# A recurrent attention kernel with a MoE layer behind it: the old state added on TensorE, the range check gathered at the end, two more slabs inverted by halves, a new tile order, and an issue order read from a table

## The chip, the cores and the metric

One core of one Trainium2 chip. The metric is the device time of one launch in microseconds (us). The kernel before takes 695.13 us, the median of three runs (693.57 to 698.21).

## The reference

For each of 4 x 8 batch heads a state of 40 x 40 is carried over 768 steps, then a normalised two-layer block with a residual follows on the 320 joined channels of each position:

```python
for t in range(S):
    y[:, :, t] = einsum('bhd,bhde->bhe', rt, state)
    Sa = einsum('bhde,bhe->bhd', state, at)
    state = state * wt[:, :, None, :] - einsum('bhd,bhe->bhde', Sa, bt) + einsum('bhd,bhe->bhde', vt, kt)
xn = (x - mu) / sqrt(var + 1e-6) * g_ln          # x: y of all heads, [4, 768, 320]
out = x + maximum(xn @ w_ch1, 0) @ w_ch2         # 320 -> 1280 -> 320
```

## The kernel before

The 768 positions are 24 chunks of 32; all 32 batch heads of a chunk are worked on together. Seven **slabs** group the chunks: 0-1, 2-3, 4-7, 8-11, 12-15, 16-19, 20-23.

**prep(c)** loads the chunk's decays and inputs (`load_e`, L332, two transfers of some 450 KB into `wa` and `bk`), forms the running products of the decays with two scans on DVE (`gE` L356, `qE` L365), multiplies `aT` (L373) and `bk` (L387) by them, checks the range of the decays (`wild`, L345), transposes `qE` (pq, L398) and multiplies all pairs of positions (`tri`, L412); the product, masked on DVE (`gk`, L419), goes to DRAM (`d_g`). **invert(slab)** reads a slab's triangles back, one per partition, solves them by substitution in 30 steps (or, for slabs in `HALVES`, two halves side by side in 14), each step a multiply and an add (L465, L471, L475), and stores the result (`d_tt`). Slabs 0 to 2 are inverted on DVE, 3 to 6 on POOL.

**chain(c)** is the recurrence: prh (L549, needs the state), a copy `hv` on ACT, solve (L564, with the slab's inverse `tt`; in chunks of `HALVES` three solves with a copy between, the middle one with `nn`), four copies `u` into `x` (L579) and one into `ub`, then st (L596): the update of the state in two PSUM banks. Four DVE additions (L606) add the old state while they move it to the other state buffer, and for 12 of the 23 next chunks, those where the frame of the products starts anew, four more DVE instructions scale it (L614). ss (L628) transposes the state. **post(c)** makes the outputs: ut (L653), z (L672) and its mask on DVE (L681), y (L693), `xt` (L701). After each odd chunk, **norm(g)** (statistics on DVE and ACT, transposes nt, L874) and **moe(g)** follow for 256 positions: ten first-layer blocks of 8 matmuls (L925), each followed by a relu on ACT (`hh`, L930) and a remainder on DVE (`hl`, L934), and twenty second-layer blocks of 3 matmuls (L902). A pair of chunks and its MoE block are called a pair below; there are 12.

tri and z take their matmuls in groups of four: the operands stand in two halves of the rows (`HROW`), the results go to two halves of the columns.

**The order.** Every step is entered as a task with an assumed duration and with what it reads and writes. `Plan.run` lays all tasks on the five engines in one pass of list scheduling: whichever ready task has the earliest due time goes next, MoE blocks get due times 37 us apart (`PERIOD`), and where PE has nothing ready between 6 and 70 us of the plan, it gets a filler matmul (`unit`, L1036). The instructions are then emitted in that order, engine by engine; each engine runs its own in order. All transfers are issued by SP's queue, in order.

```python
        by_time = sorted(order)
    with tc.manual_schedule():
        for at, _, t, b in by_time:
            if t is unit:
                unit(b)
            else:
                t["emit"](t["on"], b)
```

After the last task the collected range check is folded (L1052, L1054, L1058, L1060) and read by all engines; only if a decay was out of range a slow loop runs, which it does not here.

Of the kernel before, what the change touches and what calls it, by code (L numbers as in the profile page):

```python
# [11 lines left out]
F32 = mybir.dt.float32  # L12
# [20 lines left out]
HALVES = (0, 1)  # L33
BY_POOL = (3, 4, 5, 6)
NBK = 7
NPI = 10
NXT = 5

PERIOD, END = 18.5, 500.0
STRETCH = 1.5  # L40
UNITS = (6.0, 70.0)
BACKLOG = 2.0
RATE = 270.0


class Plan:

    ENGINES = ("PE", "DVE", "ACT", "POOL", "SP")  # L50
    READ = {"PE": 0.28, "DVE": 0.09, "ACT": 0.11, "POOL": 0.12}
# [26 lines left out]
    def run(self, n_banks=8, unit=None):  # L78
        T = self.tasks
        n = len(T)  # L80
        follow = [[] for _ in T]
        left = [0] * n
        uses = {}
        opens = {k: t for t in T for k in t["bank"]}
        for t in T:
            for k in t["ps"]:
                o = opens[k]
                if o is not t:
                    o["deps"].update(d for d in t["deps"] if d < o["n"])
        for t in T:  # L90
            for d in t["deps"]:
                follow[d].append(t["n"])
            left[t["n"]] = len(t["deps"])
            t["uses"] = set()
        for t in T:
            for k in t["bank"]:
                uses[k] = 0
        for t in T:
            for k in t["ps"]:
                uses[k] += 1  # L100
        free = {e: 0.0 for e in self.ENGINES}
        ready = {e: [] for e in self.ENGINES}
        ends = [None] * n
        avail = [0.0] * n
        done = [False] * n
        banks = list(range(n_banks))
        held = {}
        count = {"moe": 0, "po": 0, "small": 0}
        cap = {"moe": 2, "po": 2, "small": 5}
        wire = [0.0]  # L110
        events = []
        order = []
        now = 0.0

        def release(t):
            for e, us in t["where"]:
                heapq.heappush(ready[e], (t["key"], t["n"]))

        for t in reversed(T):
            us = min(u for _, u in t["where"])  # L120
            if t["where"][0][0] == "SP":
                us = 0.45 + t["kb"] / RATE + t["land"] + 1.0
            else:
                us = us * STRETCH + 0.3
            late = t["due"] if t["due"] is not None else min((T[f]["late"] for f in follow[t["n"]]), default=END)
            t["late"] = late - us
            t["key"] = t["late"] + t["shift"]
        for t in T:
            if left[t["n"]] == 0:
                release(t)  # L130
        events.append(0.0)
        n_done = 0
        back = []
        while n_done < n:
            while back and back[0][0] <= now + 1e-9:
                heapq.heappush(banks, heapq.heappop(back)[1])
            moved = True
            while moved:
                moved = False
                for e in self.ENGINES:  # L140
                    if free[e] > now + 1e-9 or e == "SP" and wire[0] > now + BACKLOG:
                        continue
                    put = []
                    got = None
                    q = ready[e]
                    while q:
                        k, i = heapq.heappop(q)
                        t = T[i]
                        if done[i]:
                            continue  # L150
                        if avail[i] > now + 1e-9:
                            put.append((k, i))
                            continue
                        if t["bank"]:
                            s = t["sort"] or "small"
                            if len(banks) < len(t["bank"]) or count[s] + len(t["bank"]) > cap[s]:
                                put.append((k, i))
                                continue
                        got = t
                        break  # L160
                    for x in put:
                        heapq.heappush(q, x)
                    if got is None:
                        if e == "PE" and unit and UNITS[0] <= now < UNITS[1] and banks:
                            order.append((now, len(order), unit, heapq.nsmallest(1, banks)[0]))
                            free[e] = now + 0.3
                            heapq.heappush(events, free[e])
                        continue
                    t, i = got, got["n"]
                    us = dict(t["where"])[e]  # L170
                    done[i] = True
                    n_done += 1
                    for k in t["bank"]:
                        s = t["sort"] or "small"
                        count[s] += 1
                        held[k] = (heapq.heappop(banks), s)
                    t["on"] = e
                    t["at"] = now
                    order.append((now, len(order), t, {k: held[k][0] for k in t["ps"]}))
                    free[e] = now + us  # L180
                    if e == "SP":
                        start = max(wire[0], now + us)
                        wire[0] = start + t["kb"] / RATE
                        heapq.heappush(events, wire[0] - BACKLOG + 1e-3)
                        end = wire[0] + t["land"]
                    else:
                        end = now + us
                    t["end"] = end
                    heapq.heappush(events, free[e])
                    heapq.heappush(events, end)  # L190
                    for k in t["ps"]:
                        uses[k] -= 1
                        if not uses[k]:
                            b, s = held[k]
                            count[s] -= 1
                            heapq.heappush(back, (end + 0.1, b))
                            heapq.heappush(events, end + 0.1)
                    for f in follow[i]:
                        left[f] -= 1
                        lag = 0.0 if e == "SP" else self.READ[e]  # L200
                        fe = T[f]["where"]
                        if len(fe) == 1 and fe[0][0] == e:
                            lag = 0.0 if e != "PE" else 0.0
                        if e == "SP":
                            lag = 0.1
                        avail[f] = max(avail[f], end + lag)
                        if not left[f]:
                            heapq.heappush(events, avail[f])
                            release(T[f])
# [981 lines left out]
```

## Time and profile before

| | |
|---|---|
| median of three runs | 695.13 us |
| the profiled execution, its own time | 701.11 us |
| its span (first to last instruction) | 699.4 us |
| mean granted TensorE clock, as a share of 2.4 GHz | 0.82 |
| busy: PE, DVE, ACT, POOL | 588.6, 433.7, 280.1, 254.6 us |
| moved by DMA | 92.13 MB |

Matmuls are pipelined, so PE's busy time includes latencies that overlap; the distance from the start of one group to the start of the next says what a group costs. The granted clock of a stretch is 1.00 at 2.4 GHz and 0.50 at 1.2 GHz. A matmul of full fp32 stands as two records in the trace and as one instruction in the program.

### The profile page before, as it was taken

How to read it: one execution, taken by the hardware profiler on the slowest of the kernel's cores; microseconds unless marked ns; L12 is line 12 of the kernel's file. 1: busy time of each engine (PE TensorE's matmuls, PEld its weight loads, DVE VectorE, ACT ScalarE, POOL GpSimd, SP SyncE). 2: the span in 40 equal slices, each digit the busy share in tenths (PEclk: the TensorE clock that was granted, in tenths of full speed). 3: DMA queues.
4: the chain of work that ended last, by engine and by line, in shares of the span. 5: the costliest groups of instructions: out<-in, count | busy, mean ns of one | idle time of the engine just before them, and what ended most of it. 6: DMA issues, size and time to landing. Idle time of an engine off the chain costs nothing.

```text
span 699.4 us, 29631 instructions
## 1 busy us (share of the span) xinstructions
PE 588.6 (84%) x13160; PEld 535.1 (77%) x13160; DVE 433.7 (62%) x923; ACT 280.1 (40%) x672; POOL 254.6 (36%) x357
## 2 busy tenths in 40 slices
PE   7998777479979779699798888897896998989976
PEld 6897676368868679599688787796795987969865
DVE  7798967699977657654585656654436355263422
ACT  7432336623334533443524424423425335253321
POOL 8427522452149923088411157711088000000000
PEclk9999865559989769869699699697697795977969
DMA  8898679644393765563566556256424242050100
GB/s 250 211 240 184 183 184 223 188 131 123 109 190 92 198 145 176 157 154 84 155 145 176 131 119 192 69 125 168 85 60 134 54 146 63 18 149 1 34 1 23
DMA packets 90549, 92.13 MB, mean 132 GB/s; under 512 B 55728, under 2 KB 70064, under 8 KB 90416
## 3 DMA queue, kind: packets, MB, share of 16 engines
q1 hardware_dynamic: 90416, 90.18, 50.0%
q8 instruction: 105, 1.72, 1.1%
q14 instruction: 28, 0.23, 0.1%
HBM read 71.11 MB, written 19.05 MB: 129 GB/s over the span
## 4 chain that ended last, share of the span: by engine, by line
PE 66%; DVE 21%; issue 7%; ACT 2%; DMA 2%; SPq 0%; DVEq 0%; ACTq 0%
PE ps L925 17%; PE ps L902 14%; PE ps L564 4%; PE ps L412 4%; PE ps L672 4%; PE ps L549 3%; PE ps L1036 3%; PE ps L628 3%; PE ps L693 3%; DVE x L614 2%; PE ps L596 2%; PE ps L398 2%; PE ps L521 2%; PE ps L874 2%; PE ps L653 2%
## 5 line engine op out<-in xcount | busy, mean ns | idle before, releaser
L925 PE MATMUL ps<-xh,w 128*128 128x256 f32 x480 | 123.1, 317 | 4.7 <-DVE xl L882 1.8
L930 ACT ACTIVATE hh<-ps 128x256 fp32r<-128x256 f32 x120 | 46.1, 385 | 173.1 <-PE ps L925 172.2
L934 DVE SCALAR_TENSOR_TENSOR hl<-ps,hh 128x256 fp32r<-128x256 f32 x120 | 50.1, 421 | 100.9 <-ACT hh L930 100.5
L902 PE MATMUL ps<-w,hh 128*128 128x320 f32 x480 | 111.6, 318 | 0.0
L925 PEld LDWEIGHTS ps<-xh,w 128*128 128x128 f32 x480 | 95.4, 219 | 7.3 <-ACT xh L878 2.2
L387 POOL TENSOR_TENSOR bk<-bk,gE 112x1024 f32<-112x1024 f32 x24 | 56.8, 2369 | 75.9 <-DMA d_g<-gk 22.7
L902 PEld LDWEIGHTS ps<-w,hh 128*128 128x128 f32 x480 | 77.3, 188 | 1.7
L925 PE MATMUL ps<-xl,w 128*128 128x256 f32 x240 | 74.8, 311 | 0.0
L902 PE MATMUL ps<-w,hl 128*128 128x320 f32 x240 | 74.0, 308 | 0.0
L475 POOL TENSOR_TENSOR yi<-yi,ytmp 128x30 f32<-128x30 f32 (+14 forms) x120 | 65.7, 547 | 9.4
L471 POOL TENSOR_TENSOR ytmp<-yi 128x30 f32<-128x30 f32 (+14 forms) x120 | 65.3, 544 | 8.6
L681 DVE TENSOR_TENSOR x5s<-ps,mask 64x256 f32<-64x256 f32 x96 | 40.5, 422 | 37.7 <-PE ps L672 35.9
L1036 PE MATMUL ps<-start,ident 128*128 128x160 f32 x318 | 54.7, 330 | 8.6 <-DVE gk L419 5.4
L373 POOL TENSOR_TENSOR aT<-wa,qE 112x512 f32<-112x512 f32 x21 | 27.3, 1302 | 94.0 <-DVE qE L365 43.1
L527 ACT COPY xk<-ps 64x320 f32<-64x320 f32 x96 | 40.4, 420 | 45.3 <-PE ps L521 44.0
L1036 PEld LDWEIGHTS ps<-start,ident 128*128 128x128 f32 x318 | 49.6, 211 | 10.4 <-DVE gk L419 5.9
L925 PEld LDWEIGHTS ps<-xl,w 128*128 128x128 f32 x240 | 52.7, 219 | 0.6 <-DVE xl L882 0.5
L606 DVE TENSOR_TENSOR x<-ps,x 40x320 f32<-40x320 f32 x92 | 45.0, 489 | 7.5 <-PE ps L596 5.5
L635 ACT COPY xk<-ps 40x320 f32<-40x320 f32 x92 | 38.6, 420 | 17.4 <-PE ps L628 11.3
L902 PEld LDWEIGHTS ps<-w,hl 128*128 128x128 f32 x240 | 45.1, 188 | 0.0
L628 PE MATMUL ps<-ident,x 40*104 40x40 f32 x368 | 30.8, 249 | 15.9 <-DVE x L614 14.4
L628 PEld LDWEIGHTS ps<-ident,x 40*104 40x104 f32 x368 | 25.5, 154 | 24.1 <-DVE x L614 10.5
(115 smaller groups left out, 1138.4 us busy)
## 6 DMA issues: line engine op xcount, KB each, us to landing
rvu<-in_rv_dram SPq DMA_DIRECT2D x24, 672.0 KB
wa<-in_et_dram SPq DMA_DIRECT2D x24, 455.4 KB
bk<-in_et_dram SPq DMA_DIRECT2D x24, 448.0 KB
d_g<-gk SPq DMA_DIRECT2D x48, 128.0 KB
x<-in_vt_dram SPq DMA_DIRECT2D x48, 128.0 KB
d_a<-aT SPq DMA_DIRECT2D x24, 231.0 KB
x2s<-d_a SPq DMA_DIRECT2D x48, 99.0 KB
x5s<-in_r_dram SPq DMA_DIRECT2D x48, 96.0 KB
```

Source lines behind the costliest of these rows:

```text
L387: (nc.gpsimd if e == "POOL" else nc.vector).tensor_tensor(out=kb, in0=kb, in1=ge[R, :, 0:C].unsqueeze(2).broadcast_to([112, 16, 2, C]), op ...
L471: g.tensor_tensor(out=tv, in0=y[:, j + 1:, j:j + 1].broadcast_to([n, m, j]), in1=y[:, j:j + 1, 0:j].broadcast_to([n, m, j]), op=ALU.mult)
L475: g.tensor_tensor(out=yv, in0=yv, in1=tv, op=ALU.add)
L527: nc.scalar.copy(out=xk[c % 2][64 * pp:64 * pp + 64, pp, 4 * z:4 * z + 4], in_=banks[b[name]][64 * pp:64 * pp + 64].rearrange("p (i f x) - ...
L606: nc.vector.tensor_tensor(out=x2[n][bs, pp, hf, :, 0:D], in0=banks[b[names[pp]]][64 * hf:64 * hf + D, 0:CH].rearrange("p (h e) -> p h e", ...
L628: nc.tensor.transpose(out=banks[b[name]][0:104, D * k:D * k + D], in_=X2[bs, pp, hf, 2 * h:2 * h + 2].rearrange("p h e -> p (h e)")[:, 0:104],
L681: nc.vector.tensor_tensor(out=x5s[zs, pp].rearrange("p f h t -> p (f h) t")[:, par::2], in0=banks[b[f"pz{c}_{par}"]][zs, 0:256].rearrange( ...
L902: nc.tensor.matmul(banks[b[name]][:, 0:CH], lhsT=l[:, us], rhs=ws[f"w2_{f}"][:, y], start=f == 0 and x == 0, stop=f == 9 and x == 2)
L925: nc.tensor.matmul(ph, lhsT=l, rhs=r, start=x == 0, stop=x == 7)
L930: nc.scalar.activation(out=hhs[n], in_=banks[b[name]][:, 0:256], func=AF.Relu)
L934: nc.vector.scalar_tensor_tensor(out=hls[n], in0=banks[b[name]][:, 0:256], scalar=0.0, in1=hhs[n].bitcast(F32), op0=ALU.max, op1=ALU.subtract)
L1036: nc.tensor.matmul(banks[b][:, 0:160], lhsT=ident, rhs=flat(start0)[:, 0:160], start=True, stop=True)
```

## The change

- The state's old value is added in PSUM by TensorE: `se` multiplies it by the identity into the two banks of st before st accumulates there. What DVE did in L606 becomes a copy on ACT or DVE, or, in frame chunks, one DVE multiplication from PSUM that replaces L606 and L614.
- The range check leaves prep: at the end eight transfers of 480 KB (`ww`, all decays once more) and eight DVE instructions do it for all chunks, folded and flagged inside the ordered part.
- Slabs 2 and 3 (chunks 4 to 11) are inverted by halves.
- `aT`, `bk`, the inversion steps and some weight conversions may be put on DVE or POOL each; the conversions get buffers of their own.
- tri and z take their four tiles in the order of `TILES`.
- `Plan.run` is gone; the order, the engine of each task and its PSUM banks are read from a table of 2,689 words. It has no filler matmuls.

```diff
-HALVES = (0, 1)
-BY_POOL = (3, 4, 5, 6)
+HALVES = (0, 1, 2, 3)
-NPI = 10
+NPI = 8
+TILES = ((0, 0), (1, 1), (1, 0), (0, 1))
 class Plan:
-    def run(self, n_banks=8, unit=None):
...
+    def listed(self, table):
         held = {}
...
+        for word in table.split():
+            n = word.rstrip("0123456789")
+            if n == "u":
+                yield None, "PE", int(word[1:])
+                continue
+            cut = next(i for i, x in enumerate(word) if x.isalpha())
+            t = self.tasks[int(word[:cut])]
+            held.update(zip(t["bank"], map(int, word[cut + 1:])))
+            yield t, self.ENGINES[word[cut]], {k: held[k] for k in t["ps"]}
...
-        task(both, a_, r=[kw, kq], w=[("aT", c % 2)], of="aT")
+        task([("DVE", 0.68), ("POOL", 1.18)], a_, r=[kw, kq], w=[("aT", c % 2)], of="aT")
...
-        task([("DVE", 1.25), ("POOL", 2.35)] if c < 4 else [("POOL", 2.35)], kb_,
-             r=[kg], w=[kbk], of="kb")
-        task([("DVE", 0.7)], wild_, r=[kw], w=["wild"], of="wild")
+        task([("DVE", 1.25), ("POOL", 2.2)], kb_, r=[kg], w=[kbk], of="kb")
...
             for i in range(8):
-                for pp in range(2):
-                    for hf in range(2):
+                for hf, pp in TILES:
...
-            task(eng, step, 2 * (lo + per * N), w=[ky], of="inv")
+            task([("DVE", 2 * (0.15 + 1.25e-3 * N)), ("POOL", 2 * (0.15 + 2.4e-3 * N))], step, w=[ky], of="inv")
...
+        if c and c + 1 < NCH:
+            def se(e, b):
+                for pp in range(2):
+                    bs = slice(BAND[pp], BAND[pp] + D)
+                    for hf in range(2):
+                        nc.tensor.matmul(
+                            banks[b[names[pp]]][64 * hf:64 * hf + D, 0:CH], lhsT=ident[bs, bs],
+                            rhs=X2[bs, pp, hf, :, 0:D], start=True, stop=False)
+            task("PE", se, 0.6, r=parts + ["ident"], w=["se"], bank=names, of="se")
...
-                                rhs=X2[zs, pp, hf, h, 0:D], start=True, stop=True)
+                                rhs=X2[zs, pp, hf, h, 0:D], start=c == 0, stop=c == 0 or h == 7)
...
                     def ev(e, b, hf=hf, bs=bs, pp=pp):
-                        nc.vector.tensor_tensor(
-                            out=x2[n][bs, pp, hf, :, 0:D],
-                            in0=banks[b[names[pp]]][64 * hf:64 * hf + D, 0:CH].rearrange("p (h e) -> p h e", e=D),
-                            in1=X2[bs, pp, hf, :, 0:D], op=ALU.add)
-                    task("DVE", ev, 0.49, r=[("x2", i, "s", hf, pp)], ps=[names[pp]], w=[("x2", n, "s", hf, pp)], of="st")
-                if frame:
-                    for hf in range(2):
-                        def sc(e, b, bs=bs, pp=pp, hf=hf):
-                            (nc.gpsimd if e == "POOL" else nc.vector).tensor_tensor(
-                                out=x2[n][bs, pp, hf, :, 0:D], in0=x2[n][bs, pp, hf, :, 0:D],
-                                in1=x2s[n][bs, pp, hf, 256:264].unsqueeze(2).broadcast_to([D, 8, D]), op=ALU.mult)
...
+                        src = banks[b[names[pp]]][64 * hf:64 * hf + D, 0:CH].rearrange("p (h e) -> p h e", e=D)
+                        dst = x2[n][bs, pp, hf, :, 0:D]
+                        if frame:
+                            nc.vector.tensor_tensor(
+                                out=dst, in0=src, in1=x2s[n][bs, pp, hf, 256:264].unsqueeze(2).broadcast_to([D, 8, D]),
+                                op=ALU.mult)
+                        else:
+                            (nc.scalar.copy if e == "ACT" else nc.vector.tensor_copy)(out=dst, in_=src)
...
-                    for pp in range(2):
-                        for par in range(2):
+                    for par, pp in TILES:
...
-    ms = [yi[1].rearrange("p i x -> p (i x)")[:, CH * i:CH * i + CH].bitcast(U32) for i in range(3)]
+    ms = [stat.tile([128, CH], F32, name=f"ms{i}").bitcast(U32) for i in range(3)]
...
+    def range_check():
...
+        for i in range(8):
+            t = wa[i % 2]
+            dma(lambda i=i, t=t: sync.dma_start(out=t[:, 0:n], in_=ww[i]), 492, w=[("wa", i % 2)], of="ww")
+            def wild(e, b, t=t):
+                nc.vector.scalar_tensor_tensor(
+                    out=v, in0=t[:, 0:n].bitcast(U32), scalar=0x3f000000, in1=v,
+                    op0=ALU.bitwise_xor, op1=ALU.bitwise_or)
...
-    order = plan.run(unit=unit)
-    by_time = sorted(order)
     with tc.manual_schedule():
-        for at, _, t, b in by_time:
+        for t, e, b in plan.listed(TABLE):
...
+TABLE = """
+5d 13a 6g 35s 14d 20s 10d 2d 21s 7g 12a 0d 3d 36s 11g 37d 15a 72s 4g 282s 8g 16a 22d 18g 69s 500s 23d 27g 24d 26a 41a
...
```

Three places show how the order moves. On PE in the late part (before, the end of chunk 19 and the start of chunk 20; after, chunk 21): `x` is the state, `bk` and `xk` the chunk's inputs, `xn` the normalised rows, `w` with `hh` and `hl` the second MoE layer. Before:

```order
L521 MATMUL ps_66<-ident,bk_90 128x104 x4
L693 MATMUL ps_67<-xk_97,x5s 32x40 x32
L521 MATMUL ps_66<-ident,bk_84 128x104 x4
L521 MATMUL ps_68<-ident,bk_84 128x104 x4
L628 MATMUL ps_66<-ident,x_0_91 104x40 x8
L549 MATMUL ps_67<-x_0_91,x2s_93 32x40 x32
L874 MATMUL ps_66<-ident,xn_132 128x128 x3
L628 MATMUL ps_68<-ident,x_0_91 104x40 x8
L564 MATMUL ps_67<-hv_99,tt_115 32x40 x32
L874 MATMUL ps_69<-ident,xn_132 128x128 x3
```

and after:

```order
L755 MATMUL ps_68<-w_2_1109,hh_138 128x320 x2
L755 MATMUL ps_68<-w_2_1109,hl_141 128x320
L390 MATMUL ps_67<-x_1_94,x2s_96 32x40 x32
L421 MATMUL ps_70<-x_1_94,ident 40x320 x2
L421 MATMUL ps_69<-x_1_94,ident 40x320 x2
L480 MATMUL ps_66<-ident,x_1_94 104x40 x8
L405 MATMUL ps_71<-hv_101,tt_118 32x40 x32
L727 MATMUL ps_72<-ident,xn_132 128x128 x3
L755 MATMUL ps_73<-w_0_1038,hh_139 128x320 x2
L755 MATMUL ps_73<-w_0_1038,hl_142 128x320
L755 MATMUL ps_73<-w_1_958,hh_137 128x320 x2
L755 MATMUL ps_73<-w_1_958,hl_140 128x320
```

Before, a pair's chain, transposes and normalisation follow one another with no MoE matmul among them; after, MoE blocks of the pair before stand on both sides of each step of the chain.

On SP at the head, up to the loads of the first inverse (`tt`): `wa` are the chunks' decays, `r` weights, `d_a`, `d_g` and `d_tt` go through DRAM. Before:

```order
L498 DMA tt_115<-d_tt_182 128x1x256
L332 DMA wa_82<-in_et_dram 112x1041
L433 DMA d_a_155<-aT_108 112x528
L732 DMA r_1_1_928<-in_w_dram 128x256
L732 DMA r_1_2_936<-in_w_dram 128x256
L498 DMA tt_116<-d_tt_182 128x1x256
```

and after:

```order
L589 DMA r_9_796<-in_w_dram 128x320
L274 DMA d_g_177<-gk 64x512 x2
L278 DMA d_a_158<-aT_111 112x528
L187 DMA wa_85<-in_et_dram 112x1041
L274 DMA d_g_177<-gk 64x512 x2
L318 DMA d_tt_182<-yi_113 64x32x32
L187 DMA wa_84<-in_et_dram 112x1041
L278 DMA d_a_157<-aT_110 112x528
L339 DMA tt_117<-d_tt_182 128x1x256
```

The last weights and the decays of chunk 8 now stand ahead of the first `tt`; before, it came ahead of chunk 6's decays and of half of the weights.

On DVE in the late part: `hl` are MoE remainders, `x5s` z's mask. Before:

```order
L606 TENSOR_TENSOR x_0_91<-ps_70,x_1_92 40x8x40 x2
L606 TENSOR_TENSOR x_0_91<-ps_71,x_1_92 40x8x40 x2
L701 TENSOR_TENSOR xt_131<-ps_67,pi_126 128x320
L837 BN_STATS st<-xt_131 128x6
L841 BN_AGGR mv_147<-st 128x2
L845 TENSOR_SCALAR sm_149<-mv_147 128x2
L614 TENSOR_TENSOR x_0_91<-x_0_91,x2s_93 40x8x40 x2
L851 RECIPROCAL sm_149<-sm_149 128x2
```

and after:

```order
L787 SCALAR_TENSOR_TENSOR hl_140<-ps_73,hh_137 128x256
L462 TENSOR_TENSOR x_0_93<-ps_67,x2s_95 40x8x40
L787 SCALAR_TENSOR_TENSOR hl_142<-ps_72,hh_139 128x256
L552 TENSOR_TENSOR xt_128<-ps_68,pi_119 128x320
L462 TENSOR_TENSOR x_0_93<-ps_69,x2s_95 40x8x40 x2
L797 SCALAR_TENSOR_TENSOR ot_143<-ps_71,xt_129 128x320
L797 SCALAR_TENSOR_TENSOR ot_144<-ps_70,xt_130 128x320
L462 TENSOR_TENSOR x_0_93<-ps_67,x2s_95 40x8x40
L879 SCALAR_TENSOR_TENSOR bk_89<-wa_84,bk_89 128x960
```

The state took eight DVE instructions with the statistics of the normalisation between them; now it takes four, with MoE work between them, and range-check instructions (L879) stand among them.

## Rows read from the trace of the kernel before

**Rows 1.** Stretches: length, busy per engine (and instructions), granted clock, DMA share, GB/s.
```profile
0.00:71.34 71.34, 61.81 (x967) 57.01 (x967) 59.66 (x98) 32.10 (x65) 41.79 (x52) 0.98 0.84 223
71.34:145.45 74.11, 50.29 (x1520) 44.07 (x1515) 57.77 (x129) 37.83 (x95) 26.76 (x30) 0.60 0.71 184
...
145.45:668.32 522.87, 453.58 (x10532) 412.64 (x10533) 309.89 (x682) 204.08 (x498) 186.02 (x277) 0.83 0.47 119
...
668.32:699.40 31.08, 22.93 (x148) 21.43 (x148) 6.35 (x15) 6.07 (x15) 0.00 (x0) 0.83 0.04 13
```

**Rows 2.** Waits of PE from 145.45 to 668.32: total us, times, longest.
```profile
PE ps L628 <- DVE x L614: 11.2, 9, 1.9
PE ps L549 <- DVE x L614: 7.8, 8, 2.0
PE ps L412 <- issue: 6.7, 4, 2.2
...
PE ps L693 <- issue: 1.3, 2, 0.7
```

**Rows 3.** The stretches of Rows 1's view inside one late pair.
```profile
582.00:594.00 12.00, 11.67 (x223) 10.23 (x222) 4.77 (x11) 5.76 (x14) 0.00 (x0) 0.50 0.21 63
...
596.00:616.00 20.00, 20.00 (x396) 18.86 (x398) 7.24 (x17) 5.58 (x14) 0.00 (x0) 1.00 0.23 67
```

**Rows 4.** Timeline of PE, one late pair: start, us, line, operands, records.
```profile
567.72 0.79 PE L564 MATMUL ps<-hv,tt 32*32 32x40 f32 x64
568.44 0.56 PE L902 MATMUL ps<-w,hh 128*128 128x320 f32 x2
568.84 0.31 PE L902 MATMUL ps<-w,hl 128*128 128x320 f32 x1
...
570.25 0.64 PE L653 MATMUL ps<-ident,ub 128*104 128x128 f32 x4
570.82 0.83 PE L628 MATMUL ps<-ident,x 40*104 40x40 f32 x16
571.59 1.13 PE L672 MATMUL ps<-rvu 40*64 40x32 f32 x64
572.54 0.49 PE L596 MATMUL ps<-x,xk 64*40 64x40 f32 x30
```

**Rows 5.** Timeline of PE early, where the granted clock is 1.00.
```profile
18.25 0.76 PE L398 MATMUL ps<-ident,qE 104*32 104x80 f32 x32
18.94 0.94 PE L521 MATMUL ps<-ident,bk 104*128 104x104 f32 x8
19.71 2.90 PE L1036 MATMUL ps<-start,ident 128*128 128x160 f32 x20
22.55 1.13 PE L412 MATMUL ps<-aT,bk 40*64 40x32 f32 x64
...
86.60 0.82 PE L596 MATMUL ps<-x,xk 64*40 64x40 f32 x64
87.26 1.14 PE L412 MATMUL ps<-aT,bk 40*64 40x32 f32 x64
88.32 0.64 PE L653 MATMUL ps<-ident,ub 128*104 128x128 f32 x4
```

**Rows 6.** Two MoE steps of the chain that ended last: start, us, records.
```profile
315.28 1.89 PE ps L925 x16
317.17 1.76 PE ps L902 x12
```

**Rows 7.** DVE's scaling of the state, by line; and two timeline rows of DVE.
```profile
L614 DVE TENSOR_TENSOR x<-x,x2s 40x320 f32<-40x320 f32 x48 | 25.5, 563 | 0.7
...
45.98 0.26 DVE L465 TENSOR_TENSOR ytmp<-yi 64x108 f32<-64x108 f32 x1
...
72.62 4.70 DVE L345 SCALAR_TENSOR_TENSOR wild<-wa,wild 112x512 uint32<-112x512 uint32 x1
```

**Rows 8.** SP's queue: the wait that costs it most, total us, times, longest.
```profile
SPq L489 <- PE ps L549: 106.8, 17, 18.5
```

More of the change, by code (lines that the diff above doesn't have):

```diff
@@ L76, in add @@
         return t["n"]
-    def run(self, n_banks=8, unit=None):
[L79 to L106, printed above, removed]
-        held = {}
[L108 to L209, printed above, removed]
-                    moved = True
-            nxt = None
-            while events:
-                x = heapq.heappop(events)
-                if x > now + 1e-9:
-                    nxt = x
-                    break
-            if nxt is None:
-                if n_done < n:
-                    stuck = [(t["of"], t["n"], left[t["n"]], t["bank"]) for t in T if not done[t["n"]]]
-                    raise RuntimeError(f"the plan stands at {now}: {stuck[:12]} {count} {banks}")
-                break
-            now = nxt
-        return order
@@ L369, in prep @@
         a = aT[c % 2]
-        both = [("DVE", 0.72), ("POOL", 1.45)] if c < 4 else [("POOL", 1.45)]
         def a_(e, b):
@@ L446, in invert @@
             r=[("d_g", si, k) for k in range(len(SLABS[si]))], w=[ky], of="y_in", land=4.0)
-        eng = "POOL" if by_pool else "DVE"
-        g = nc.gpsimd if by_pool else nc.vector
         def ones(e, b):
@@ L461, in step @@
             def step(e, b, j=j, m=m, N=N):
+                g = nc.gpsimd if e == "POOL" else nc.vector
                 if half:
@@ L587, in chain @@
         if c + 1 < NCH:
-            names = [f"pst{c}_{pp}" for pp in range(2)]
             def st(e, b):
@@ L768, in e2 @@
                     hi = words(i)[1].bitcast(F32)
-                    nc.gpsimd.tensor_tensor(out=m.bitcast(F32), in0=m.bitcast(F32), in1=hi, op=ALU.mult)
-                task("POOL", e2, 0.85, r=[("raw", i), ("yi", 1)], w=[("m", i % 3)], of="w")
+                    (nc.gpsimd if e == "POOL" else nc.vector).tensor_tensor(
+                        out=m.bitcast(F32), in0=m.bitcast(F32), in1=hi, op=ALU.mult)
+                task([("POOL", 0.75), ("DVE", 0.43)], e2, r=[("raw", i)], w=[("m", i % 3)], of="w")
             else:
@@ L961, in setup @@
         task("DVE", starts, 0.8, w=["start0"], of="setup")
+        task("DVE", lambda e, b: nc.vector.memset(ones, 1.0), 0.1, w=["ones1"], of="setup")
         def starts1(e, b):
@@ L1011, in until, with zero, fold, whole @@
             listed += 1
+    def range_check():
+        key = ("bk", NCH % NBK)
+        acc = bk[NCH % NBK]
+        n = NCH * C * 10 // 8
+        v = acc[:, 0:n].bitcast(U32)
+        def zero(e, b):
+            (nc.gpsimd if e == "POOL" else nc.vector).memset(v, 0)
+        task([("POOL", 1.0), ("DVE", 0.6)], zero, w=[key], of="wz")
+        for i in range(8):
[5 more added lines that the diff above has]
+                    op0=ALU.bitwise_xor, op1=ALU.bitwise_or)
+            task("DVE", wild, 1.2, r=[("wa", i % 2)], w=[key], of="wild")
+        def fold(e, b):
+            nc.vector.tensor_scalar(out=v, in0=v, scalar1=24, scalar2=None, op0=ALU.logical_shift_right)
+            nc.vector.tensor_reduce(out=any_w, in_=v, axis=mybir.AxisListType.X, op=ALU.max)
+        task("DVE", fold, 1.6, r=[key], w=["any"], of="fold")
+        def whole(e, b):
+            nc.tensor.matmul(banks[b["flag"]][0:1, 0:1], lhsT=any_w, rhs=ones, start=True, stop=True)
+        task("PE", whole, 0.2, r=["any", "ones1"], bank="flag", of="flag")
+        def flag_(e, b):
+            nc.vector.tensor_scalar(
+                out=flag, in0=banks[b["flag"]][0:1, 0:1], scalar1=0.0, scalar2=None, op0=ALU.is_gt)
+        task("DVE", flag_, 0.2, ps=["flag"], w=["flagged"], of="flag")
     until(0)
@@ L1120 @@
+"""
 _OUT = (NCH, 128, CH)
```

244 lines of the change are left out of this document (182 added, 62 removed).

## The prediction

> **What bounds the kernel now.** I cut the span at four places that both programs have: the first solve, the first MoE matmul, the normalisation of the last pair, the end. The view of stretches gives each its share [rows 1]. Ahead of the first solve (71 us) the DMA engines are busy 0.84 of the time at 223 GB/s; up to the first MoE matmul (74 us) DVE is busy 57.8 us and the granted clock of PE is 0.60; then come 523 us with the MoE blocks, PE busy 454 us of them; then 31 us for the last block alone.
>
> The long stretch decides. Its work can be priced from starts on the timeline where the clock is 1.00. A solve takes 0.72 us (567.72 to 568.44), ut 0.57, ss of a chunk 0.77, z 0.95 [rows 4]; prh and y have as many matmuls as solve, of the same width, and go at its price. A chunk's pq takes 0.69, its input transposes (L521) 0.77, tri 1.06 (87.26 to 88.32), st 0.66 [rows 5]. Eight matmuls of the first MoE layer take 0.94 (16 in 1.89), three of the second 0.44 (12 in 1.76) [rows 6], so a block of 10 and 20 such groups takes 18.2. The nt transposes I estimate at 0.42 a group. Counted along PE's order between the two marks, before: 11 blocks 200, nt 8, chain and output steps (23 solves, 21 prh, 21 st, 21 z, 22 y, 21 ut, 42 halves of ss, 40 halves of transposes) 125, pq and tri 15 times each 26. That is 360 us. Going from small tiles to full ones costs more: two L902 matmuls after a solve take 0.40 (568.44 to 568.84) [rows 4] where they take 0.29 inside a run [rows 6], so some 0.1 a switch; with 140 switches 14.
>
> So 523 us hold 374 of work at 2.4 GHz, 69 in which PE is idle (522.9 less 453.6), and 79 that only the lower clock explains: at 0.83 a third of the stretch, 174 us, runs at 1.2 GHz, and half of that is 87. Of the idle time 19 is waiting for DVE to scale the state (L614), and 24 stands as "issue" (six rows, the first and the last shown) [rows 2].
>
> Where the clock falls is seen in a late pair: from 582 to 594 it is 0.50 although PE is busy 11.7 of 12 us; from 596 to 616, with MoE and chain mixed, it is 1.00 [rows 3]. What PE did before it fell is the run without MoE matmuls. The order has ten such runs, each 7 to 12 us of work, about 107 us together, one between any two MoE blocks.
>
> **The change, part by part.**
>
> *Long stretch, work.* The same count along the new order: MoE 196, nt 8, chain and output steps with 36 solves (the halves of slabs 2 and 3 add two a chunk) and z at its new price 126, pq and tri 20. tri and z in the new tile order: the nearest row is st, which alternates its column half at every matmul as TILES does, with 64 records in 0.66 [rows 5]; the old order changed columns at every second one and took 1.06 and 0.95. I take 0.70 for both; the ends are 0.66 and the old prices. The addition of the old state is new: four fp32 matmuls of 320 columns. Ten of 160 columns take 2.84 one after the other [rows 5], so one of 320 takes 0.57; the four stand in four different quarters of the array. Side by side they cost 0.57, in series 2.27; st gets through 32 matmuls of 40 columns in 0.66 where L1036's pace gives 2.3, so I take 0.66, 19 times 12.5 us. Sum 363. Switches: 229, 23 us.
>
> *Long stretch, waiting and clock.* The wait for L614 goes: a frame chunk has four DVE instructions from PSUM instead of eight, one after the other saving 4 x 0.563 = 2.3 us [rows 7]; other chunks share four copies between ACT and DVE. What is late next is those copies, and behind st there now stand MoE blocks, so PE has work. Normalisation is hidden the same way. I keep "issue" at 24 and half of the other 26, 37 us. Of the runs without MoE three are left (7, 9.5 and 11 us, 27 together), so of the 79 us of low clock a quarter, 20. The new order mixes everywhere else, as 596 to 616 did. Sum 363 + 23 + 37 + 20 = 443, which is 80 less.
>
> *Head.* SP's order now puts 23.6 MB ahead of the first inverse: 10 loads of decays, 9 of inputs, all 21 of weights, and the chunks' own traffic. Before, it was 15.3 MB. At the 223 GB/s of that stretch [rows 1] this is 106 us, so the first solve comes 35 us later. Ends: 89 us, if the busy share of 0.84 became 1, and 128 at the 184 GB/s of the next stretch. The filler matmuls vanish; PE waits there anyway, and their cover, a warm clock in the first chunk, is worth little against DMA.
>
> *First solve to first MoE matmul.* Four chunks instead of three. DVE's 57.8 us lose 17 inversion steps of 2 x 0.26, the 8 scalings at 0.563 and one range check that took 4.70 [rows 7], 18 together, and gain copies and conversions, some 7: 46. Before, the stretch was 1.28 times DVE's time; so 59. Ends: 46, and 74 if four chunks go no faster than three did.
>
> *End.* The last block's transposes are done inside the block before; 23.5 us of dense work and some 6.5 us to the last landing make 30, against 31. The range check's eight DVE instructions stand among late work where DVE is not the bound, and its transfers fall where DMA has room: 0, with the end at 8 times 2 us if one held `hl` back.
>
> *Other edits.* POOL has 254.6 us of work, less than half of it needed at a time; moving steps between it and DVE I cost at nothing, covered by the long stretch, in which DVE is busy 310 of 523 us. If that cover went, the price is DVE's wait for POOL seen at 72.62.
>
> **Sum.** 106 + 59 + 443 + 30 = 638 us of span against 699.4; with the 1.7 us around it 640, against the profiled execution's own 701.1. That execution lies 6 us above the median of the runs shown, so 634 in medians.
>
> The tile order is where a rule speaks against the change. In rows, st has neighbours that share a row half, and takes 0.66. The Trainium skill (TensorE: Matmul & The Clock Gate, "Part 3: Packing small matmuls — row/col tiling") says that a weight load overlaps running matmuls only when its row group differs. The old order changed row halves every time; the new one keeps them at every second step. By that rule tri and z would gain nothing, by st's row they gain 15 us.
>
> **Rivals.** (1) *The forecast*, 605 to 660: chance 0.44. (2) *Dense*: loads keep the DMA engines fully busy and no clock is lost: 89 + 46 + (363 + 23 + 24) + 30 = 575, 571 in medians, and up to 605. For it: mixed stretches ran at 1.00 without a gap. Against: "issue" waits come whatever the order. 0.25. (3) *The clock keeps falling* between sparser MoE groups: 60 of the 79 us stay, 674. For it: 582 to 594 was cold while PE was busy. 0.15. (4) *Row halves bind*: tri and z keep their old price, because neighbours that load weights into the same half wait for each other: 634 + 15 = 649. Against: st. 0.08. (5) *Slower, through SP's queue*: a load whose buffer is still being read holds up all behind it. Before, L489 waited for prh 17 times, 106.8 us, 6.3 each [rows 8]; PE hardly noticed, since loads ran ahead. In the new order each chunk's loads stand closer to their use. If one such stall a pair reached PE, 12 x 6.3 = 75 us make 709; it is slower than before from eleven on (703). 0.08.
>
> **How the numbers follow.** A measurement tells about 1% from no change, that is 688 to 702. Faster by more: all of 1, 2 and 4 and most of 3 (0.11), 0.88. Within 1%: 0.05, from 3 and 5. Slower: 0.07. The range 578 to 690 leaves out the low end of 2, and 5: the high end also covers se in series (35 us).
>
> **What would show it.** Right: the first solve later than 90 us; granted clock above 0.9 in the long stretch; no wait of PE for the scaling; tri and z at about 0.7; se near 0.7. Wrong: the first solve before 80 us, a clock below 0.85 with MoE mixed in, se near 2.3, or PE waiting for DMA in the long stretch.

## The result, and the profile after

The changed kernel takes 671.7 us (median of 4; before, on the same chip, 694.35). Counted over undisturbed runs it takes 0.959 of the time before, 95% interval 0.951 to 0.967: about 28 us faster, where 61 were forecast. The profiled execution takes 665.3 us, its span 663.6, against 638 in the sum.

The stretches of [rows 1] in the changed kernel, cut at the same four places (first solve, first MoE matmul, nt of the last pair, end; same columns):

```profile
0.00:97.27 97.27, 30.46 (x848) 26.70 (x849) 56.66 (x83) 30.23 (x61) 53.07 (x87) 1.00 0.91 243
97.27:166.53 69.26, 51.42 (x1711) 41.41 (x1711) 46.39 (x98) 43.25 (x110) 32.63 (x55) 0.71 0.50 124
166.53:633.99 467.46, 432.96 (x11311) 388.81 (x11308) 260.45 (x593) 212.15 (x533) 136.45 (x206) 0.93 0.53 137
633.99:663.60 29.61, 23.55 (x180) 23.29 (x178) 8.06 (x18) 6.28 (x16) 0.00 (x0) 0.98 0.07 25
```

Forecast were 106, 59, 443 and 30. The first MoE matmul comes at 166.5 (165 forecast) and the end takes what it should. The miss is in the long stretch: 24 us too long, though the clock did rise, 0.83 to 0.93, and PE's idle time halved, 69.3 to 34.5.

PE's waits in that stretch, the group that answers to [rows 2]:

```profile
PE ps L405 <- issue: 6.2, 5, 2.3
PE ps L244 <- issue: 4.5, 3, 3.0
PE ps L257 <- issue: 4.0, 2, 3.3
PE ps L405 <- DMA tt<-d_tt: 3.5, 1, 3.5
```

The waits for the scaling of the state (19 us) are gone. What is left is nearly all "issue", 28 of 34 us.

PE's timeline where the clock is 1.00, the rows that answer to [rows 4, 5]: L257 is tri, L523 z, L421 the new se, L544 y, L405 a solve.

```profile
279.64 1.14 PE L257 MATMUL ps<-aT,bk 40*64 40x32 f32 x64
280.71 0.56 PE L755 MATMUL ps<-w,hh 128*128 128x320 f32 x2
...
597.24 1.14 PE L523 MATMUL ps<-rvu 40*64 40x32 f32 x64
598.19 0.73 PE L421 MATMUL ps<-x,ident 40*40 40x320 f32 x8
598.85 0.56 PE L755 MATMUL ps<-w,hh 128*128 128x320 f32 x2
...
600.36 0.80 PE L544 MATMUL ps<-xk,x5s 104*32 104x40 f32 x64
601.09 0.79 PE L405 MATMUL ps<-hv,tt 32*32 32x40 f32 x64
601.81 0.56 PE L755 MATMUL ps<-w,hh 128*128 128x320 f32 x2
```

From start to start, se takes 0.66 (forecast 0.66), y 0.73, a solve 0.72. tri takes 1.07 and z 0.95 (mostly 1.06 elsewhere): the new order of the quarters has brought nothing.

Where the clock falls now, in stretches around two pauses (same columns as the stretches above):

```profile
198.00:203.40 5.40, 5.36 (x213) 4.67 (x200) 2.73 (x11) 2.48 (x6) 0.00 (x0) 1.00 0.75 207
203.40:205.76 2.36, 0.02 (x3) 0.00 (x0) 0.24 (x1) 0.00 (x0) 0.00 (x0) 0.85 0.96 251
205.76:215.00 9.24, 9.24 (x207) 8.34 (x208) 4.53 (x9) 3.61 (x11) 2.20 (x1) 0.50 0.27 85
215.00:226.00 11.00, 11.00 (x347) 9.97 (x345) 4.77 (x10) 4.95 (x12) 3.39 (x2) 0.99 0.36 100
```
```profile
234.00:240.50 6.50, 6.19 (x237) 5.16 (x226) 4.99 (x10) 4.00 (x11) 0.00 (x0) 1.00 0.59 150
240.50:243.80 3.30, 0.06 (x3) 0.00 (x0) 0.35 (x2) 1.44 (x5) 0.00 (x0) 0.82 1.02 280
243.80:249.00 5.20, 5.18 (x164) 4.77 (x167) 2.59 (x9) 0.84 (x2) 1.17 (x1) 0.50 0.21 54
```

PE is busy at 1.00, stands for 2.4 and 3.3 us, and comes back at 0.50 although it is then busy without a gap. All nine falls of the clock in the long stretch come in or within 2 us behind a pause of PE, of 0.8 to 3.5 us. The same holds before, for 16 falls. The reverse does not hold: of the changed kernel's 15 pauses of 0.8 us or more seven, up to 2.0 us long, have no fall behind them. Here is the fall before that leads to the cold late pair of [rows 3]:

```profile
574.00:578.50 4.50, 4.46 (x114) 3.85 (x113) 3.26 (x8) 1.99 (x5) 0.00 (x0) 0.62 0.76 219
578.50:579.84 1.34, 0.01 (x1) 0.03 (x1) 1.24 (x5) 1.28 (x5) 0.00 (x0) 1.00 0.52 151
579.84:582.00 2.16, 1.18 (x14) 0.85 (x14) 1.96 (x9) 1.29 (x4) 0.00 (x0) 0.76 0.04 10
```

I had started reading at 582, saw PE busy at 0.50, and blamed the run without MoE matmuls. The pause stands 3.5 us ahead of it.

### The profile page after: what moved, and what is told of

The parts are those of the page before. It is cut to its first block, busy times and chain, and to the rows that moved or that the text cites. A ratio compares the mean times of both kernels' runs of the same rounds, so it can differ in the third digit from the quotient of the medians.

```text
span 663.6 us, 31287 instructions
## 1 busy us (share of the span) xinstructions
PE 538.4 (81%) x14042; PEld 480.2 (72%) x14042; DVE 371.6 (56%) x792; ACT 291.9 (44%) x720; POOL 222.2 (33%) x346
## 4 chain that ended last, share of the span: by engine, by line
PE 71%; DMA 12%; issue 6%; ACT 4%; DVE 3%; SPq 3%; POOL 1%; DVEq 0%; ACTq 0%; POOLq 0%
PE ps L778 18%; PE ps L755 17%; PE ps L405 6%; PE ps L523 4%; PE ps L362 3%; PE ps L480 3%; PE ps L390 3%; PE ps L257 3%; PE ps L544 3%; PE ps L446 3%; DMA nn<-d_g 3%; PE ps L421 3%; DMA wa<-in_et_dram 2%; PE ps L505 2%; DMA tt<-d_tt 2%
## 5 line engine op out<-in xcount | busy, mean ns | idle before, releaser
L236 POOL TENSOR_TENSOR bk<-bk,gE 112x1024 f32<-112x1024 f32 x20 | 45.5, 2275 | 89.4 <-DVE gE L206 44.2
L316 POOL TENSOR_TENSOR yi<-yi,ytmp 128x108 f32<-128x108 f32 (+25 forms) x120 | 64.3, 536 | 9.4
L244 PE MATMUL ps<-ident,qE 104*32 104x80 f32 x768 | 24.8, 282 | 44.4 <-DVE qE L215 39.9
L244 PEld LDWEIGHTS ps<-ident,qE 104*32 104x32 f32 x768 | 18.6, 135 | 48.5 <-DVE qE L215 30.8
L312 POOL TENSOR_TENSOR ytmp<-yi 128x184 f32<-128x184 f32 (+14 forms) x75 | 39.3, 524 | 32.0 <-DVE yi L316 27.4
L405 PE MATMUL ps<-hv,tt 32*32 32x40 f32 x2304 | 35.6, 221 | 15.5 <-DMA tt<-d_tt 8.0
L405 PEld LDWEIGHTS ps<-hv,tt 32*32 32x32 f32 x2304 | 30.2, 125 | 24.3 <-issue 13.0
L257 PE MATMUL ps<-aT,bk 40*64 40x32 f32 x1536 | 36.8, 252 | 13.2 <-issue 11.5
L257 PEld LDWEIGHTS ps<-aT,bk 40*64 40x64 f32 x1536 | 33.6, 172 | 18.3 <-issue 14.4
L206 DVE TENSOR_TENSOR_SCAN gE<-wa,start 112x528 f32<-112x528 f32 x24 | 32.8, 1367 | 21.1 <-DMA wa<-in_et_dram 21.1
```

Of the source, the lines that this page charges most:

```text
L236: (nc.gpsimd if e == "POOL" else nc.vector).tensor_tensor(out=kb, in0=kb, in1=ge[R, :, 0:C].unsqueeze(2).broadcast_to([112, 16, 2, C]), op ...
L244: nc.tensor.matmul(o[32 * bb:32 * bb + 32, j], lhsT=qe[R4, 4 * j + bb, 1:33], rhs=sel, start=True, stop=True)
L257: nc.tensor.matmul(pg[64 * pp:64 * pp + 64, i], lhsT=tb[rs, 64 * p:64 * p + 64], rhs=a[rs, pp, C * i:C * i + C], start=True, stop=True)
L312: g.tensor_tensor(out=tv, in0=y[:, j + 1:, j:j + 1].broadcast_to([n, m, j]), in1=y[:, j:j + 1, 0:j].broadcast_to([n, m, j]), op=ALU.mult)
L316: g.tensor_tensor(out=yv, in0=yv, in1=tv, op=ALU.add)
L405: nc.tensor.matmul(o[qs, h], lhsT=mat[qs, h], rhs=vec[qs, h], start=True, stop=True)
```

## The experiments

Each is compared with the kernel before on its own chip; the changed kernel stands at 0.959.

**1. The old order of the quarters.**

```
-TILES = ((0, 0), (1, 1), (1, 0), (0, 1))
+TILES = ((0, 0), (1, 0), (0, 1), (1, 1))
```


> The changed kernel with the old order of the four quarters in tri and z, nothing else. Theory A (the forecast's): the order of the quarters sets their price, so tri (24) goes from what it is to 0.36 us more and z (24) to 0.25 to 0.3 us more, together 14 to 16 us slower. Theory B: the price goes by something both orders share (in the trace after, tri still takes 1.07 us and z 0.95 to 1.06), so within 3 us of the changed kernel, and tri and z keep 1.07 and 0.95 to 1.06.

670.1 us, ratio 0.964 (0.955 to 0.973): the changed kernel's time. tri still takes 1.06 from start to start:

```profile
279.26 1.14 PE L257 MATMUL ps<-aT,bk 40*64 40x32 f32 x64
280.32 0.56 PE L755 MATMUL ps<-w,hh 128*128 128x320 f32 x2
```

The order is worth nothing; theory B.

**2. The disputed costs by themselves.** Series of small matmuls, ahead of all and behind all:

```
+def mm(row, col, K, M, N): ...
+    out=banks[b + row][64*col:64*col+M, 0:N], lhsT=ident[rows, 0:M], rhs=ident[rows, 0:N]
```


> The changed kernel with eight series of small fp32 matmuls put on PE's queue twice, on the identity and with results that nobody reads: once at the start, where PE waits for the first loads and the DMA engines are busy, and once behind the last block, where no load runs. Seven series of 64 matmuls (128 records): weights 64 wide in the new order, in the old order, always the same quarter; then in the new order weights 40 wide, 32 wide, then 64 rows with weights and columns 40 as in st, then weights 64 wide with 64 columns. The eighth: 1024 matmuls as in st. Theory A (order sets the price): the old order takes 2.1 us, the new one 1.4. Theory B (the width of the weights sets it): both 2.1, same quarter no faster; 40 wide 1.3; 32 wide 1.05 to 1.4. For the pauses that the profile calls issue: theory C (PE's instructions are fetched by DMA, and a fetch comes late when small matmuls use them up fast while loads fill the DMA engines): the eighth series shows pauses of 1 to 3 us at the start and shorter ones or none at the end. Theory D (the pauses come from waits that the profile doesn't see): no pauses in either, since this series waits for nothing. The whole program 25 to 45 us longer.

842.6 us in its one run: 171 more than the changed kernel, where 25 to 45 were expected; with its pauses the eighth series alone took 57 us at the end, and it stands in the program twice. PE's timeline of the series, the first four rows at the start, the others at the end (L933 64-wide weights in the new order, L936 in the old one, L939 always the same quarter, L942 40 wide, L945 32 wide, L948 the series behind it):

```profile
1.44 3.64 PE L933 MATMUL ps<-ident 40*64 40x32 f32 x128 [1.44 <-POOL sign L828]
4.87 2.76 PE L936 MATMUL ps<-ident 40*64 40x32 f32 x95
10.97 1.08 PE L936 MATMUL ps<-ident 40*64 40x32 f32 x33 [3.33 <-issue]
11.85 13.73 PE L939 MATMUL ps<-ident 40*64 40x32 f32 x127
...
766.29 2.42 PE L942 MATMUL ps<-ident 40*40 40x32 f32 x123
768.65 1.06 PE L945 MATMUL ps<-ident 40*32 40x32 f32 x59
770.66 1.18 PE L945 MATMUL ps<-ident 40*32 40x32 f32 x69 [0.95 <-issue]
771.77 1.28 PE L948 MATMUL ps<-ident 64*40 64x40 f32 x59
```

From start to start a record costs 27 ns with weights 64 wide, in the new order (128 in 3.43 us) and in the old (33 in 0.88); 106 in the same quarter every time (127 in 13.4); 19 with weights 40 wide and 16 with 32 (123 in 2.36, 69 in the 1.11 to the next series). These rows ran at the low clock's price; at the high clock tri's records take 17 ns and a solve's, 32 wide, 11. So tri and z are dear for the width of their weights, and both orders that change the quarter cost the same. The eighth series (64 rows, 40 wide), then the DMA share in it:

```profile
795.23 2.37 PE L954 MATMUL ps<-ident 64*40 64x40 f32 x128 [1.10 <-issue]
798.70 2.37 PE L954 MATMUL ps<-ident 64*40 64x40 f32 x128 [1.10 <-issue]
802.44 2.37 PE L954 MATMUL ps<-ident 64*40 64x40 f32 x128 [1.37 <-issue]
```
```profile
800.00:820.00 20.00, 12.91 (x705) 12.02 (x696) 0.00 (x0) 0.00 (x0) 0.00 (x0) 0.50 0.02 4
```

A pause behind every 128 records, with the DMA engines at 0.02: neither C nor D as written. Matmuls that wait for nothing pause without any load beside them. At the start, too, the loads had ended before this series (share 0.02 from 30 to 60 us), so it says nothing of what loads add. A block of 128 records, with its weight loads 256 instructions, comes every 3.5 to 4 us, and what uses it up sooner waits. The DMA part of the changed kernel's page (queue, packets, MB, share) has the blocks:

```profile
q8 instruction: 111, 1.82, 1.1%
```

14,042 matmuls and as many weight loads in 111 packets are 253 a packet; in the trace each packet has 16,384 bytes.

**3. Fillers where PE waits early.** 37 `u` entries in the table, ahead of ten steps (`+u1 u1 u1 u1` ahead of the first ut, and so on).

> The changed kernel with 37 filler matmuls (0.28 us each) at ten places of PE's queue between the first solve and the first MoE matmul, ahead of steps that waited there. Theory E (a pause of PE lowers the clock, and the cold 40 us before the first MoE matmul cost 15 to 20): the clock stays at 1.00 from 104 to about 160 and the time falls by 8 to 18 us. Rival F (that stretch is set by copies, conversions and loads, PE waits for them at either clock): the clock may rise, the time changes by less than 4 us.

687.0 us, ratio 0.985 (0.972 to 0.997): slower. Its stretch from first solve to first MoE matmul took 71.0 us against 69.3, though 35 us of it are recorded at the high clock, against 10 (solves of 0.79 us stand among those of 1.29). E's condition was met in part only, for the clock fell three times in it, but the time did not fall with what was gained: F fits better. Some 15 us were lost later, in the long stretch (483 us), with nothing edited there. So where do pauses fall?

**4. se undone.** No matmuls for the old state; DVE adds it (30 copies move from ACT to DVE for that).

```
-nc.tensor.matmul(..., lhsT=ident[bs, bs], rhs=X2[bs, pp, hf, :, 0:D], start=True, stop=False)
+nc.vector.tensor_tensor(out=dst, in0=src, in1=X2[bs, pp, hf, :, 0:D], op=ALU.add)
```


> The changed kernel with the first part undone: no se on PE, the four copies of each new state become additions of the old state on DVE, and in frame chunks a multiplication behind each. Theory G (the forecast's): se costs PE 0.66 x 22 = 14.5 us, and its absence puts 88 DVE instructions more or longer ones (about 0.56 us each) back on the way to the next chunk; waits of PE for them come back, 10 to 30 us, so 0 to 15 us slower. Rival H: PE is the bound now and the MoE pieces cover DVE, so 8 to 14 us faster.

695.2 us, ratio 0.995 (0.990 to 0.9997): nearly all that the change had gained is gone. G was right in sign and too small. PE's waits in its long stretch, and that stretch:

```profile
PE ps L390 <- DVE x L465: 6.6, 7, 1.4
```
```profile
171.20:662.74 491.54, 442.61 (x11158) 404.19 (x11156) 290.17 (x661) 200.56 (x504) 138.28 (x204) 0.90 0.50 131
```

PE waits 19 us for other engines and loads (5.7 in the changed kernel), its idle time is 49 us, and 102 us run at the low clock, not 66. se costs PE 12.5 us and saves more than twice that. Yet this long stretch is still 31 us shorter than the one before: the rest of the change gained that, and its later start of the MoE work (171.2 for 145.5) spends 26 of it.

**5. The blocks shifted.** 16, 32 and 48 fillers at the start of PE's queue (`+u0 u0 ...` ahead of the first transposes), where PE waits anyway.

> The changed kernel with 16 filler matmuls (32 records) at the very start of PE's queue, where PE waits 40 us for its first transposes; all else as it was. Theory C, as the series at the end of the last run left it (PE's instructions come in blocks of 256, that is 128 matmul records with their weight loads, one block per 3.5 to 4 us, and a block used up faster ends in a pause): every pause called issue lies at a block's end, so all of them move to 32 records earlier in the order, other steps are hit, and the time changes by chance, up to 15 us either way, with the cold stretches that follow the pauses. Rival D (the pauses belong to the steps in which they stand): the same steps pause as in the changed kernel, and the time stays within 3 us of it.

> As the shift by 32 records, with 32 filler matmuls (64 records). Theory C: the pauses lie 64 records earlier in the order than in the changed kernel; time up to 15 us either way. Rival D: the same steps as in the changed kernel, the time within 3 us of it.

> As the shift by 32 records, with 48 filler matmuls (96 records). Theory C: the pauses lie 96 records earlier in the order than in the changed kernel (32 later, counted from the next block); time up to 15 us either way. Rival D: the same steps as in the changed kernel, the time within 3 us of it.

Medians 675.5, 689.9 and 677.8 us; ratios 0.973 (0.965 to 0.981) for 32 records and 0.977 (0.969 to 0.984) for 96. By an edit that takes no time of its own the kernel shifted by 64 is slower: its four times run from 679 to 692, the changed kernel's from 665 to 678. For 32 that is not clear of the noise, since the two intervals overlap, and for 96 just clear. The 37 early fillers of experiment 3 are 74 records, so they shifted the blocks too, which may be where their 15 us went; no run tells that apart. One pause of the changed kernel, and one of the kernel shifted by 32, at nearly the same place:

```profile
203.08 0.34 PE L405 MATMUL ps<-hv,tt 32*32 32x40 f32 x14
205.76 1.14 PE L405 MATMUL ps<-hv,tt 32*32 32x40 f32 x50 [2.34 <-issue]
```
```profile
200.25 0.82 PE L405 MATMUL ps<-hv,tt 32*32 32x40 f32 x64
203.14 0.69 PE L505 MATMUL ps<-ident,ub 128*104 128x128 f32 x4 [2.06 <-issue]
```

The pause has left the middle of the solve for the step ahead of ut. For the issue pauses I counted the program's own matmul records ahead of each on PE's queue; the remainders by 128 at five places, in order of time:

| kernel | remainders (at about 200, 240, 330, 396, 440 us) |
|---|---|
| changed | 75, 69, 59, 51, 45 |
| shifted by 32 | 43, 37, 26, 20, 12 |
| shifted by 64 | 10, 4, 122, 116, 112 |
| shifted by 96 | 109, 103, 90, 83, 78 |

At each place a row lies 28 to 34 below the one above it (counted by 128). The slow fall along a row fits what other instructions on PE's queue take up. All 24 issue pauses of the changed kernel's long stretch lie on such a line, from 79 down to 29, and each of them ends 1.2 to 1.7 us after a packet of the instruction queue has landed; so do those of the shifted kernels and the 19 of the kernel before. Theory C in its corrected form is shown, D refuted. What loads beside a packet add is not tested by itself.

**6. MoE steps mixed in to thin out the blocks.** 95 moves in the table.

> The changed kernel with 95 moves of MoE steps (each by at most twelve places on PE, nothing else moved) that put full-size matmuls between small ones, so that fewer blocks of 128 records run in under 4 us. Priced by a pause of 3.5 us less the block's own time (a mean over where blocks may begin) the pauses behind the first MoE matmul sum to 23.7 us in the changed kernel (28.4 were measured) and 18.3 here. Theory C: issue pauses 4 to 8 us fewer, fewer cold stretches, 5 to 20 us faster. Rival I (moved MoE steps wait for their own inputs on DVE): other waits of PE grow by as much, within 5 us or slower.

667.8 us, ratio 0.963 (0.954 to 0.973): the changed kernel's time. In the profiled execution (679.5 us, 12 above that median) issue pauses in the long stretch fell from 28 to 20 us, as theory C has it, but other waits rose from 6 to 19, the largest new ones for copies on ACT that the moved steps now queue up with:

```profile
PE ps L505 <- ACT ub L437: 4.3, 5, 1.5
...
PE ps L778 <- ACT x L431: 2.8, 2, 1.8
```

Rival I.

**7. Later weight loads, three eased waits, both, and no range check.** The first moves 12 loads in SP's order behind the first inverse, one by one; the first pair of lines shows two of them, 95s and 94s, leave their places. The other lines are the second, whole but for the cuts:

```
-270s 95s 90s 94s 51g
+270s 90s 51g
...
-1395s 689p ... 1001s      -1124p2 ... 821p3      -608a 212g 392a 702s 592a 591a 594d 941p5 593a 938d 595a
+1001s 1395s 689p ...      +... 821p3 1124p2      +212g 392a 702s 592a 591a 594d 941p5 593a 938d 595a 608a
```


> The changed kernel with 12 of the 21 weight loads (3.5 of the 24.0 MB that stand ahead of the first inverse on SP's queue) moved to where their conversions begin, behind the load of the first inverse. Theory J (the forecast's head: loads set the time of the first solve): at 243 GB/s the first solve comes 14.6 us earlier, at 83 instead of 97, and the first MoE matmul up to as much earlier, 5 to 14 us in all. Rival K (the inversion steps on DVE and POOL set it, or the conversions then wait for their loads and hold DVE and ACT): the first MoE matmul stays within 3 us of 166.5.

> The changed kernel with three of its waits on loads eased: the load of the inverse of chunk 8 ahead of two transfers on SP's queue, the solve that waited 3.5 us for it behind one more MoE step, and ACT's scaling of a landed block (it had held the copies that ut waited 3.6 us for) behind those copies. Theory (a pause costs its own length and the cold stretch behind it, and is worth more than its length): 7 us of waits go, and with them half of the 20 us that run cold behind them, 8 to 17 us faster. Rival (what waited is late anyway, and the clock falls at the next pause): 0 to 4 us.

> Both edits of the two kernels before it, the later weight loads and the three eased waits. If they are independent: the sum of the two.

> The changed kernel without the eight loads of the range check (3.8 MB) and its eight DVE instructions; the flag is computed from zeros. The forecast priced the check in its late place at 0, at most 16 us: within 3 us of the changed kernel. Rival (its loads hold SP's queue or DVE late in the program): 4 us or more faster.

Ratios 0.966 (0.957 to 0.975), 0.960 (0.951 to 0.969), 0.961 (0.952 to 0.970) and 0.964 (0.954 to 0.974): four times the changed kernel's time, where 5 to 14 and 8 to 17 us had been expected of the first two. The check is worth 0, as forecast. With the loads moved the first solve came at 92.5, 5 us earlier and not 15, and the first MoE matmul at 165.2, so K holds. Its rows from the start to the first solve:

```profile
0.00:60.00 60.00, 20.77 (x560) 18.24 (x560) 34.41 (x46) 24.14 (x46) 31.99 (x53) 1.00 0.91 237
60.00:92.54 32.54, 9.68 (x288) 8.46 (x288) 22.97 (x37) 5.94 (x15) 23.00 (x35) 1.00 0.79 185
```

Up to 60 us loads fill the DMA engines; then they have room (0.79), and DVE and POOL are busy 23 us each of 32.5. Easing three waits took 4 us off the idle time. The clock's fall behind the eased wait for tt (at 290 us) is gone with it, but another, at 235 us, now lasts 27 us where the changed kernel's, at 243, lasted 7: 85 us are low in all. No version here beats the change by more than the measurement tells.

## Why the prediction was right and wrong

**One identity carries the long stretch.** For each profiled execution I took PE's idle time and the time in which PE is busy at the low clock. What is left when the idle time and half of the busy low-clock time are taken off, in us:

| kernel | stretch | idle | busy at the low clock | left |
|---|---|---|---|---|
| before | 522.9 | 69.3 | 145 | 381 |
| changed | 467.5 | 34.5 | 63 | 402 |
| old quarter order | 471.0 | 38.2 | 61 | 402 |
| later loads | 469.8 | 33.5 | 69 | 402 |
| three waits eased | 470.7 | 30.1 | 82 | 400 |
| both | 479.9 | 33.7 | 93 | 400 |
| no range check | 473.6 | 31.3 | 85 | 400 |
| mixed | 480.0 | 38.6 | 78 | 402 |
| shifted by 32, 64, 96 | 480.1, 497.4, 479.3 | 39.3, 38.4, 43.1 | 82, 123, 67 | 400, 397, 403 |
| early fillers | 482.9 | 34.3 | 102 | 398 |
| se undone | 491.5 | 48.9 | 98 | 394 |

Kernels with the same work keep 397 to 403, whatever their time: they differ in pauses and in the clock that falls with them. In the kernel before PE was idle for 33 of its 178 us at the low clock, so that the clock cost it 73 us and not half of 178.

**Right.** The sum to the first MoE matmul (166.5 for 165), but by luck, from two errors: the head took 97 for 106, the loads having run at 243 GB/s rather than 223, and the next stretch 69 for 59. Nor do the bytes alone set the head, for with 3.5 MB less ahead of the first solve it came 5 us earlier, not 15. In the next stretch DVE was busy 46 us as forecast, but the stretch is 1.49 times that and not 1.28; what sets it stays open. The end (29.6 for 30). The waits of PE (34.5 for 37), their "issue" part staying (28 for 24). No wait for the scaling. se at 0.66. The range check at nothing. SP's queue reaching PE little: one wait for tt, 3.5 us, in the long stretch; rival 5 didn't come.

**Wrong, first step: "tri and z in the new tile order ... I take 0.70 for both".** tri takes 1.06 and z 1.04 in the mean of the rows at the high clock, so 0.36 x 15 + 0.34 x 22 = 13 us too little for the 15 tri and 22 z of the long stretch. I took st as the nearest row for its order; its weights are 40 wide, those of tri and z 64, and that is what the price follows. Rival 4 named the outcome (the old price kept) but not the cause. The Trainium skill (TensorE: Matmul & The Clock Gate, "Part 3: Packing small matmuls — row/col tiling") says that a weight load overlaps running matmuls only when its row group differs, by which neighbours in one row half would wait for each other. Experiment 2 shows that wait for one and the same quarter (106 ns a record), and not for neighbours that share only the row half: the order that has them costs what the other costs, 27 ns.

**Wrong, second step: "of the 79 us of low clock a quarter, 20".** PE was busy at the low clock for 63 us, which cost some 31, so 11 too little. The term was hung on runs without MoE matmuls; the record shows a pause of PE ahead of every fall, before and after. The change took away most waits for other engines and loads (42 us before, 6 after) and kept the pauses that come from PE's own instruction blocks (24 before, 28 after). That a pause brings the fall is read from this order in time, and from the one place in experiment 7 where the fall went with its wait; no run takes all pauses away and nothing else. Runs without MoE matmuls matter all the same, by another road: 64 records of a small step take 0.72 us, so a block of 128 is gone in 1.5, and by the 3.5 us a block a pause of 2 us can follow, an estimate.

With 2.5 us less waiting, 13 + 11 - 2.5 makes 21.5 of the 24.5 us by which the long stretch is too long; 3 us of work stay open. The 9 and 10 of the two stretches ahead nearly cancel. Of the rest of the gap between 634 and 671.7, 6 us were taken off for the profile of before standing above its median, and another 6 are how far the changed kernel's profile, its fastest run, lies below its own. Rival 3 (674) came nearest in time, by luck: it had 60 us of low clock stay, and 31 did.

**Where the gain came from.** The long stretch lost 55 us: 35 of idle time and, by half of 145 and 63 us, 41 of the clock, against 21 more of work (se 12.5, 89 more switches at 0.1, the solves of the halves, less a few MoE groups). Undoing se gives 24 of the 55 back; the other 31 belong to the rest of the change together, which no run takes apart further. The 21 us by which the first MoE matmul is late took more than a third of the gain away, so that without se nearly nothing is left. The two profiled executions lie 36 us apart, more than the 28 that all runs count.

What stays open: why the clock falls behind one pause and not behind another, and stays low for 3 us here and for 14 there; and why no edit of the order got below the changed kernel, though mixing and easing did remove some of the waits that they were made to remove.

## What to carry to other kernels

Before a stretch at the low clock is put down to the work in it, look at the rows ahead of it: in the long stretch a pause of PE stood in front of every one. Take off half of the low-clock time only where PE is busy, or idle time is counted twice. Count instructions as well as microseconds when small matmuls are packed: here a block of 128 matmul records had to last some 3.5 us, or PE waited for the next however well the rest was hidden, and edits of a few fillers far away moved the time by up to 18 us. A price taken from a neighbouring row needs the same weights' width, not only the same pattern.

## What was not expected of the hardware

- PE's instructions arrive in blocks of 256, one per 3.5 to 4 us in a series of small matmuls even with the DMA engines at 0.02; with loads beside it a pause took up to 3.3 us (share 1.02). The Trainium skill (Runtime: NRT & Kernel Launch, "Instruction fetch mechanics") gives blocks of 16 KiB, 256 instructions, and says that crossing one is mostly hidden. The size agrees with the packets of 16,384 bytes and 253 matmuls and weight loads; the hiding doesn't hold for small matmuls, with 1.1 to 1.65 us lost at each block of the series.
- The granted clock is listed as 1.00 from a program's start until its first recorded change (116 us in the changed kernel), whatever the pace. The first solves there, at 97 to 102 us, stand with 1.29 us each, the length at the low clock, against 0.79 at the high one; the eighth series took 2.37 us for 128 records both where 1.00 and where 0.50 was listed. So the 1.00 of the first stretch above is no reading, and early stretches are better read by the price of a known step.
